# Weight sums for the seven products from GpSimd to VectorE, with a new issue order in all blocks of a fused attention and feed-forward kernel

## The chip, the cores and the metric

The kernel runs on one core of a Trainium2 chip. Time is device time of one execution in microseconds (us). The core has a matrix engine (TensorE, PE in the profile; its weight loads are listed apart as PEld), a vector engine (VectorE, DVE), a scalar engine (ScalarE, ACT), GpSimd (POOL) and a queue that issues transfers (SyncE, SP). Each engine works through its own instructions in order; an instruction that has to wait holds up what stands behind it on its engine.

## The reference

```python
for c in range(24):                    # chunks of 32 queries, each with a window of keys
    k_full = concat(mem_k, k[c*32-16 : c*32+40])      # 8 memory keys and up to 56 others
    v_full = concat(mem_v, v[c*32-16 : c*32+40])
    s = q[c*32 : c*32+32] @ k_full.T / sqrt(64)
    a = exp(s - max(s));  a = a / (sum(a) + 1e-9)
    out[c*32 : c*32+32] = a @ v_full
x = attention output as (4*768, 8*64) = (3072, 512)
h = x @ w_in                           # 512 x 2048
g = where(h >= 1, h, where(h <= -1, 0, (h + 1)**2 / 4))
result = g @ w_out                     # 2048 x 512
```

Everything is float32, with 4 batches, 8 heads, 768 positions and heads of 64.

## The kernel before

The 3072 rows are six blocks of 512 (`TB`). For a block, attention makes x, transposed; then for each of 16 slices `fc` of the hidden dimension one product gives h (in PSUM, from the pool `ps_h` with two buffers), ScalarE and VectorE make g of it, and a second product adds it into the block's four output banks (two pairs, tags `a0` and `a1`). To keep float32 accuracy, every operand of a product is split into a high part (a rounded copy, by ScalarE) and a low part (the remainder, a subtraction on VectorE), and three of the four products of parts are added.

Weights come as 64-bit words; `decode` (L184) makes float32 of a pair of slices and splits it: two instructions on ScalarE, four on VectorE, of 128x1024. There are 16 such decodes, `w0` to `w15`.

Attention of half a block (`attention`, L405; for block 0 `first_attention`, L248) is a chain: scores on TensorE into the PSUM pair with tag `s`, maximum and subtraction on VectorE, exp on ScalarE, normalisation and six transposes on VectorE, the product with the values on TensorE into the same pair `s`, then high and low part of x.

Blocks 0 and 1 use plain products: `half_step` (L438; 256 rows) and `step` (L479; 512 rows). A slice of `step` passes through: h on TensorE (12 matmuls of 512 columns), relus on ScalarE (three instructions), join on VectorE, high part on ScalarE, low part on VectorE, and two output halves of six matmuls each on TensorE.

Blocks 2 to 5 (`SECOND` is 2) form h with seven products of half-size operands in place of eight (Strassen's way), four slices at a time: `quad` (L765), with `product` (L665). For that, sums of the weights are needed, once for all blocks. `build(m)` (L563), for m from 0 to 7, makes them: two additions of 128x512 join the high and the low part again (`fef`), four subtractions of 128x256 give the sums (`tf`), ScalarE splits them (`st`, a high part of 128x1024), VectorE takes the low part, and a transfer stores `st` in device memory (`saved`), from where later transfers bring it into places of the weights that are no longer needed (`load_t`, L591). `fef` and `tf` use tag `f`, which has two buffers and serves `decode` and the output copies `ob` as well. The tile `st` has one buffer. In the kernel before, the six additions and subtractions of `build` run on GpSimd.

Nothing is ordered by a scheduler while it runs. The string `FIRST` (L27) is the order in which steps of all chains of blocks 0 to 1, of the decodes, the builds and the attention of blocks 0 to 2 are issued. Each token moves its chain by one step: `g0` to `g3` are the attention of block 0, `n0` and `n1` of block 1, `n2` and `n3` of block 2; `w` are decodes; `A` and `B` half steps of the halves of block 0, `E` its steps; `C`, `D` and `F` the same for block 1; `t` are builds; `+` issues the next load of the list `early`. `n1`, `E12` and so on in this text are such chains.

`QUADS` (L61) is the order within a quad of four slices, four quads to a block, the same for each of blocks 2 to 5. `p1` to `p7` are the products, 12 matmuls of 256 columns each into the PSUM bank X or Y; `c` copies X on ScalarE, `a` adds Y on VectorE, `r`, `m`, `h`, `l` are relus, join, high and low part for one of the four parts of g, `g` adds the part into the output (12 matmuls of 512 columns). A minus sign means the part of the quad before. `z0` and `z1` copy out the two output pairs of the block before (`store`, L519: one copy on VectorE, one on ScalarE, each with its transfer). `d` and `k` are sums and splits of x, `@S` starts the attention of half of the next block and `@V` issues its value product; `0` and `1` move these attention chains by one step. All instructions stay on their engine in the order of issue (`InOrder`, L81).

Of the kernel before, what the change touches and what calls it, by code (L numbers as in the profile page):

```python
# [25 lines left out]

FIRST = """  # L27
    + + g0 g0 g0 + g0 g1 g0 + g0 g0 g1 g1 g0 g1 + g1 g0 w0 g1 g1 + g1 g0 w0 g1 w0 + g0 g1 w0 w0 g2
    + g0 w0 g1 w1 g2 + g2 g1 g0 g3 g2 + g1 g2 A0 + g3 g2 g2 g3 g2 g3 A1 A0 + g2 g2 + g3 g3 w1 A1 w2
    g3 w1 w3 A0 g3 g2 w2 g3 + g3 w1 w2 g2 + g3 g3 g2 A0 g3 B0 w1 w2 w1 w4 A0 B0 w3 A1 B0 w2 + A2 B1  # L30
    A1 A2 B1 w2 A1 w3 A0 B1 B2 + w5 w3 B1 A2 B0 B0 B2 B1 w3 w4 A3 B2 + w3 A2 w7 A2 w4 B0 w5 A1 B2
    A2 w6 w4 w5 B3 A3 B2 w4 + B1 B2 w4 E4 + A3 B3 + w8 w6 + w9 A3 w5 w5 A3 w6 w10 B3 w11 w6 w5 w7
    B3 A3 + E4 + w6 B3 E5 E4 E5 E4 w13 w7 B3 w6 w7 E4 w8 w7 w12 + E6 E5 E4 E4 E7 E5 w8 w14 + E6 E5
    E5 E5 w7 w15 w8 w9 E6 w8 w9 E6 E6 E7 w9 E6 E7 w8 w9 E6 w9 E7 E7 E8 w10 E8 E9 w11 w10 w10 E8 w10
    E8 w11 E9 E7 E8 w11 w10 w11 E8 E9 E9 E8 w12 w12 w11 E9 E10 E10 E11 w12 E7 w13 E10 w12 E10 w13 +
    n0 E10 + E11 w12 E12 E10 E12 E10 n0 w14 w13 w13 n0 E11 n0 E9 w13 E9 E11 n0 E11 n0 E11 n0 n0 +
    n0 E13 n0 n0 n0 n0 E11 n0 w14 n0 E13 w15 E12 n0 w14 n0 w15 E12 n0 E14 E12 w14 E14 n1 w14 w15
    E12 w15 n1 E15 E13 n1 E14 E13 n1 E14 E13 n1 C0 E12 n1 w15 n1 E14 n1 C0 n1 n1 n1 E15 E13 n1 C1
    E15 E13 n1 E15 E14 C1 n1 E15 C1 C2 + C0 C2 C0 C2 C1 n1 C1 E14 n1 C0 n1 E15 n1 C2 E15 C0 E15 E15
    D0 E15 C1 D1 C3 E15 t0 D0 t0 t0 t0 D3 D0 D1 t0 C2 C3 D1 D0 D1 t0 t0 t1 D0 C3 D0 C3 t0 C3 t1 t1  # L40
    D2 F4 D1 t1 D3 D2 t1 t1 D3 t1 t2 C2 D1 D2 D2 C3 D3 F5 F4 t2 t2 t2 t1 t2 D2 D2 t2 D3 F6 F4 F4 t2
    t2 F5 F5 t3 t3 t3 F4 t3 t3 F5 D3 F6 F5 F6 F5 t3 t4 F6 t3 t3 t4 F5 t4 F7 t4 n2 t4 F4 t4 t5 t5 F7
    F4 t4 F7 n2 F6 t5 t5 t4 n2 F8 F7 t5 F7 F9 t5 F8 n2 F8 F6 t6 n2 t6 t6 t5 t6 F6 F9 F8 F7 t5 t6 F8
    F9 n2 t6 t7 F7 n2 + n2 n2 F11 n2 t6 t7 t6 t7 n2 t7 t7 n2 F10 n2 F11 F9 F9 n2 F10 t7 F10 F12 t7
    F8 n2 t7 + n2 F10 F8 F10 F11 F11 n3 F13 n3 F9 n2 n3 F12 F10 n3 F11 F12 + F10 n3 n3 F12 F9 n3 n2
    n3 n3 F11 F13 n3 n3 n3 F12 F11 F14 F13 F14 n3 F12 F12 F13 n3 n3 F15 n3 + F14 F13 n3 F15 F15 F15
    F13 F15 F14 F14 F13 n3
"""


# [28 lines left out]

# [887 lines left out]
```

## Time and profile before

| | us |
|---|---|
| median of three runs | 607.29 |
| lowest and highest | 606.29, 607.94 |
| the profiled execution | 606.56 |
| its span, first to last instruction | 604.8 |
| TensorE busy, of the span | 582.8 |
| VectorE busy | 388.5 |
| ScalarE busy | 332.4 |
| GpSimd busy | 55.0 |

The profile shows one execution. A busy engine need not be at its peak: matmuls overlap, so that TensorE counts as busy while the next matmul could already have started. What it loses is seen from the distance of the starts of neighbouring matmuls. The line of an instruction is nearly always L89, that of the helper that records it; the names of the tiles tell which step it is: `ps_h` is h, `ps_o` the output, `ps_s` scores, `ps_x` values, `gw`, `gt`, `gh`, `gl` the way from h to the parts of g, `fef`, `tf`, `st` the builds, `w`, `f`, `wr` the decodes, `pr`, `pt` the probabilities and their transposes.

### The profile page before, as it was taken

To read this page: it belongs to the slowest core of one execution; us is meant where nothing else is said; L and a number is where in the kernel's file an instruction comes from. 1 tells how busy PE (TensorE), PEld (TensorE's weight loads), DVE (VectorE), ACT (ScalarE), POOL (GpSimd) and SP (SyncE) were. 2 spreads that over 40 slices of the span, in tenths; PEclk is the share of its full clock that TensorE was granted. 3 is DMA by queue.
4 is the path that set the end of the run, shared out by engine and by line. 5 is a ranking of instruction groups with operands and counts; after the bars stand their busy time and mean duration, and the time that the engine had idled before them with its cause. 6 is when DMAs were issued, how large, how long until landed. Compare 5 with 4: busy or idle time off the path is not lost.

```text
span 604.8 us, 13956 instructions
## 1 busy us (share of the span) xinstructions
PE 582.8 (96%) x6072; PEld 503.7 (83%) x6072; DVE 388.5 (64%) x547; ACT 332.4 (55%) x587; POOL 55.0 (9%) x54
## 2 busy tenths in 40 slices
...
DVE  5789999995668777744657645557555557423332
...
GB/s 353 423 418 420 23 0 106 127 59 131 166 114 244 260 74 328 179 200 161 95 72 144 170 169 165 123 72 114 200 125 86 140 3 11 199 106 92 83 0 70
DMA packets 39437, 91.07 MB, mean 151 GB/s; under 512 B 2896, under 2 KB 29776, under 8 KB 33744
## 3 DMA queue, kind: packets, MB, share of 16 engines
...
q10 hardware_dynamic: 144, 0.13, 0.1%
q14 instruction: 14, 0.11, 0.1%
...
## 4 chain that ended last, share of the span: by engine, by line
PE 83%; DVE 9%; ACT 2%; DMA 2%; POOL 2%; issue 2%; ACTq 0%; DVEq 0%; POOLq 0%
PE ps_o L89 39%; PE ps_h L89 37%; PE ps_x L89 4%; PE ps_s L89 3%; DVE pt L89 1%; DMA saved<-st 1%; POOL tf L89 1%; DVE f L89 1%; DVE gl L89 1%; DVE pr L89 1%; ACT gw L89 1%; DVE st L89 1%; DVE gw L89 1%; DVE den L89 1%; DMA qk<-in_first_qk_dram 1%
## 5 line engine op out<-in xcount | busy, mean ns | idle before, releaser
L89 PE MATMUL ps_o<-wr,gh 128*128 128x512 f32 x768 | 242.2, 396 | 2.5 <-DVE ob L89 1.6
L89 PEld LDWEIGHTS ps_o<-wr,gh 128*128 128x128 f32 x768 | 139.1, 188 | 32.3 <-DVE ob L89 2.4
L89 PE MATMUL ps_o<-wr,gl 128*128 128x512 f32 x384 | 151.9, 396 | 1.2 <-DVE gl L89 1.2
L89 PE MATMUL ps_h<-s,wr 128*128 128x256 f32 x768 | 99.7, 282 | 0.0
L89 PEld LDWEIGHTS ps_h<-s,wr 128*128 128x128 f32 x768 | 96.4, 188 | 2.5 <-ACT u L89 0.2
L89 PE MATMUL ps_h<-xth,wr 128*128 128x512 f32 (+1 forms) x320 | 92.9, 365 | 0.7 <-ACT gt L89 0.7
L89 DVE SCALAR_TENSOR_TENSOR gw<-gw,gt 128x512 f32<-128x512 f32 (+1 forms) x88 | 61.3, 699 | 47.1 <-ACT gw L89 46.5
L89 PEld LDWEIGHTS ps_o<-wr,gl 128*128 128x128 f32 x384 | 72.2, 188 | 19.1 <-DVE gl L89 2.4
L89 DVE TENSOR_TENSOR gl<-gw,gh 128x512 fp32r<-128x512 f32 (+1 forms) x104 | 71.3, 694 | 24.4 <-ACT gh L89 24.1
L89 ACT CAST gh<-gw 128x512 fp32r<-128x512 f32 (+1 forms) x104 | 60.4, 586 | 33.6 <-DVE gw L89 33.6
L89 PEld LDWEIGHTS ps_h<-xth,wr 128*128 128x128 f32 x320 | 60.1, 201 | 10.5 <-ACT gt L89 1.1
L89 ACT ACTIVATE gw<-gw 128x512 f32<-128x512 f32 (+1 forms) x104 | 61.5, 591 | 0.0
L89 DVE TENSOR_TENSOR gt<-gt,ps_h 128x512 f32<-128x512 f32 x32 | 22.0, 688 | 58.8 <-ACT gt L89 35.9
L89 PE MATMUL ps_h<-xtl,wr 128*128 128x512 f32 (+1 forms) x160 | 56.8, 364 | 0.6 <-DVE xtl L89 0.6
L89 ACT ACTIVATE gw<-ps_h 128x512 f32<-128x512 f32 (+1 forms) x56 | 29.9, 535 | 48.7 <-PE ps_h L89 39.9
L89 ACT COPY gt<-ps_h 128x512 f32<-128x512 f32 x32 | 18.7, 585 | 65.7 <-PE ps_h L89 65.7
L89 PEld LDWEIGHTS ps_h<-sa,wr 128*128 128x128 f32 x384 | 48.4, 188 | 1.8
L89 PE MATMUL ps_h<-sa,wr 128*128 128x256 f32 x384 | 49.4, 282 | 0.0
L89 DVE STREAM_TRANSPOSE pt<-pr 32x512 f32<-32x512 f32 (+1 forms) x60 | 41.4, 700 | 1.3
L89 DVE SCALAR_TENSOR_TENSOR f<-w,f 128x1024 uint32<-128x1024 uint32 x32 | 38.9, 1220 | 0.2
L89 POOL TENSOR_TENSOR fef<-wr 128x512 f32<-128x512 f32 x16 | 25.0, 1582 | 140.2 <-DMA out_dram<-ob 139.6
L89 PEld LDWEIGHTS ps_h<-xtl,wr 128*128 128x128 f32 x160 | 32.6, 204 | 5.2 <-DVE xtl L89 0.8
...
## 6 DMA issues: line engine op xcount, KB each, us to landing
...
```

Of the source, the lines that this page charges most:

```text
L89: return self.tc.keep_in_program_order(getattr(self.engine, name)(*args, **kwargs))
```

## The change

The six additions and subtractions of `build` are issued on VectorE in place of GpSimd, in the same forms. `FIRST` holds the same tokens in another order, from its 41st token on; the builds' tokens, `t0` to `t7`, stand where their steps now run in VectorE's queue. `QUADS` holds the same tokens in another order in each of its four strings. Nothing else differs. The lines of `FIRST` are cut here; the part that is kept holds the attention of block 1 (`n0`, `n1`), the first builds and the place of `n2`.

```diff
 FIRST = """
...
-    E12 w15 n1 E15 E13 n1 E14 E13 n1 E14 E13 n1 C0 E12 n1 w15 n1 E14 n1 C0 n1 n1 n1 E15 E13 n1 C1
-    E15 E13 n1 E15 E14 C1 n1 E15 C1 C2 + C0 C2 C0 C2 C1 n1 C1 E14 n1 C0 n1 E15 n1 C2 E15 C0 E15 E15
-    D0 E15 C1 D1 C3 E15 t0 D0 t0 t0 t0 D3 D0 D1 t0 C2 C3 D1 D0 D1 t0 t0 t1 D0 C3 D0 C3 t0 C3 t1 t1
...
+    E10 w12 w13 n0 E10 w13 E11 + E12 E11 w13 n0 E9 w14 n0 E10 E11 w13 E12 n0 n0 E9 E10 E11 E11 E11
+    n0 n0 E12 n0 n0 n0 n0 + E13 n0 E12 n0 w14 E13 w15 E12 w14 n0 w15 n0 n0 E14 E12 n1 w14 n0 C0 w14
+    w15 n1 E13 E15 n1 E14 E12 w15 E13 E14 E13 n1 n1 n1 E14 w15 n1 C0 E15 E14 n1 + n1 E15 n1 E13 n1
+    n1 n1 C1 n1 C1 C0 E13 E15 C2 E14 E15 E14 C1 n1 E15 n1 C2 E15 C0 n1 n1 E15 E15 C0 D0 E15 C2 E15
+    C1 D1 C3 D0 C0 C1 t0 C2 D1 D3 t0 D0 C1 D0 t0 C3 t0 D2 t0 t0 t0 D0 F5 D1 C2 t0 t1 D3 t1 t1 C3 t1
...
+    t4 F5 t5 t5 t4 t5 t5 F7 t5 n2 t5 F7 F6 t6 t5 t6 t5 F8 F8 n2 n2 F8 n2 F7 t6 F9 t6 F9 n2 t6 t6 n2
+    t6 F8 t7 n2 F8 F10 F9 F9 F6 t6 t7 F11 n2 n2 n2 F7 t7 n2 n2 + F9 t7 n2 t7 F10 F8 F11 t7 F8 t7
...
 """
...
 QUADS = (
     """
-    @S0 p1 p2 -h12 -g22 c1 p6 a11 p5 0 dS4 r11 0 m11 -l12 0 -g12 c2 kS4 p7 -g21 c3 0 a22 r22 z0 h11
-    z1 0 0 m22 h22 l11 p4 p3 r21 0 a12 l22 r12 g11 m21 h21 l21 m12
+    @S0 -h12 p1 p2 -g22 0 -l12 c1 p6 a11 0 -g12 p5 r11 0 z0 dS4 c2 m11 p7 kS4 c3 h11 a22 0 -g21 r22
+    z1 m22 l11 h22 p4 r21 0 p3 a12 l22 0 0 r12 m21 h21 l21 g11 m12
     """,
     """
-    0 p2 -h12 0 p1 c1 a11 -g21 p6 -l12 r11 m11 0 0 c2 h11 -g22 p7 p5 0 0 c3 a22 @V0 r22 -g12 p4 p3
-    0 m22 h22 l22 l11 r21 a12 r12 @S1 g11 m21 h21 l21 m12
+    p1 -h12 p2 0 0 c1 a11 0 -g21 p6 c2 -l12 0 r11 m11 0 -g22 p7 p5 0 @V0 c3 -g12 a22 h11 r22 p4 p3
+    0 m22 h22 l11 a12 r12 g11 @S1 l22 r21 m21 h21 l21 m12
     """,
     """
-    1 1 p2 p1 -g22 c1 a11 r11 1 p6 m11 1 1 -h12 p5 -g21 c2 p7 -l12 c3 h11 -g12 a22 l11 r22 m22 1 1
-    h22 p4 l22 r21 p3 1 g11 m21 h21 1 a12 r12 m12 1 1 l21
+    1 p2 p1 c1 1 a11 -g22 r11 m11 1 1 1 p6 p5 -h12 c2 -g21 p7 -l12 -g12 c3 h11 a22 1 r22 l11 m22 1
+    h22 p4 l22 r21 p3 m21 h21 1 a12 r12 m12 1 g11 1 l21 1
     """,
     """
-    p1 1 -h12 -g22 c1 p2 p6 -g21 a11 c2 -l12 1 kA11 @V1 r11 p7 1 c3 m11 h11 kA12 p5 dS3 a22 -g12
-    dS1 r22 dS2 p4 p3 l11 m22 h22 l22 kA22 a12 r21 g11 m21 r12 kS2 kS1 h21 m12 l21 kS3
+    p1 p2 c1 1 p6 -g22 -g21 c2 a11 1 kA11 @V1 r11 kA12 1 -h12 p7 m11 -l12 h11 c3 p5 dS3 a22 p4 p3
+    dS1 r22 dS2 l11 m22 h22 -g12 g11 l22 a12 kA22 r21 m21 r12 m12 h21 kS3 kS2 l21 kS1
     """,
 )
...
         for j in range(2):
             hi, lo = (weights(0, 2 * m + j, part).bitcast(F32) for part in range(2))
-            pool.tensor_tensor(fef[:, j].rearrange("p a b -> p (a b)"), hi, lo, op=ALU.add)
+            dve.tensor_tensor(fef[:, j].rearrange("p a b -> p (a b)"), hi, lo, op=ALU.add)
             yield
...
-        pool.tensor_tensor(tf[:, 1], b12, b11, op=ALU.subtract)
+        dve.tensor_tensor(tf[:, 1], b12, b11, op=ALU.subtract)
         yield
-        pool.tensor_tensor(tf[:, 2], b22, b12, op=ALU.subtract)
+        dve.tensor_tensor(tf[:, 2], b22, b12, op=ALU.subtract)
         yield
-        pool.tensor_tensor(tf[:, 0], b22, tf[:, 1], op=ALU.subtract)
+        dve.tensor_tensor(tf[:, 0], b22, tf[:, 1], op=ALU.subtract)
         yield
-        pool.tensor_tensor(tf[:, 3], b21, tf[:, 0], op=ALU.subtract)
+        dve.tensor_tensor(tf[:, 3], b21, tf[:, 0], op=ALU.subtract)
         yield
```

More of the change, by code (lines that the diff above doesn't have):

```diff
@@ L28 @@
     + + g0 g0 g0 + g0 g1 g0 + g0 g0 g1 g1 g0 g1 + g1 g0 w0 g1 g1 + g1 g0 w0 g1 w0 + g0 g1 w0 w0 g2
[L29 to L37, printed above, removed]
-    E12 w15 n1 E15 E13 n1 E14 E13 n1 E14 E13 n1 C0 E12 n1 w15 n1 E14 n1 C0 n1 n1 n1 E15 E13 n1 C1
@@ L39 @@
-    E15 E13 n1 E15 E14 C1 n1 E15 C1 C2 + C0 C2 C0 C2 C1 n1 C1 E14 n1 C0 n1 E15 n1 C2 E15 C0 E15 E15
-    D0 E15 C1 D1 C3 E15 t0 D0 t0 t0 t0 D3 D0 D1 t0 C2 C3 D1 D0 D1 t0 t0 t1 D0 C3 D0 C3 t0 C3 t1 t1
-    D2 F4 D1 t1 D3 D2 t1 t1 D3 t1 t2 C2 D1 D2 D2 C3 D3 F5 F4 t2 t2 t2 t1 t2 D2 D2 t2 D3 F6 F4 F4 t2
-    t2 F5 F5 t3 t3 t3 F4 t3 t3 F5 D3 F6 F5 F6 F5 t3 t4 F6 t3 t3 t4 F5 t4 F7 t4 n2 t4 F4 t4 t5 t5 F7
-    F4 t4 F7 n2 F6 t5 t5 t4 n2 F8 F7 t5 F7 F9 t5 F8 n2 F8 F6 t6 n2 t6 t6 t5 t6 F6 F9 F8 F7 t5 t6 F8
@@ L44 @@
[L44 to L47, printed above, removed]
+    + g0 w0 g1 w1 g2 g1 g2 g3 + g0 g2 g1 A0 g2 g3 g2 g3 + g3 A1 A0 g2 + g2 + g3 g2 g3 + A1 w1 w2 g3
+    w1 g2 w3 A0 g3 + g3 w2 g3 w1 w2 g2 + g3 g2 g2 A0 g3 g3 A1 B0 + w2 w4 w1 w1 A0 B0 w3 + A2 B0 A1
@@ new lines @@
+    w2 B1 A1 A2 + w3 B0 w2 B1 B2 B1 w4 w3 B1 w5 A2 + B1 B0 w3 A0 A3 B0 w7 A2 A1 w4 w3 A2 B2 w5 B2
+    w6 w4 + B2 w5 B2 B3 B1 A3 E4 w4 A3 + w8 w4 + B3 w5 E5 B2 w9 + A3 + E4 w6 B3 w5 A2 w6 E4 w6 B3
+    A3 A3 w5 B3 w10 w6 w7 w11 E4 B3 w6 E5 w7 w8 + w7 E5 E7 w13 w7 E5 w12 E6 + w8 w14 E4 E6 w15 w7
+    E4 w8 w9 E6 E5 E8 E5 w9 w8 w9 E6 E7 E6 w9 E7 w9 E8 E5 w8 E6 E9 E7 E7 w10 w11 w10 E7 E8 E4 E9
+    w10 E8 w10 E6 E8 w11 w10 + w11 w12 w11 E9 E7 w12 E10 w11 E9 n0 E8 E9 E8 E10 w12 E10 E11 w13 w12
+    E10 w12 w13 n0 E10 w13 E11 + E12 E11 w13 n0 E9 w14 n0 E10 E11 w13 E12 n0 n0 E9 E10 E11 E11 E11
@@ new lines @@
+    n0 n0 E12 n0 n0 n0 n0 + E13 n0 E12 n0 w14 E13 w15 E12 w14 n0 w15 n0 n0 E14 E12 n1 w14 n0 C0 w14
+    w15 n1 E13 E15 n1 E14 E12 w15 E13 E14 E13 n1 n1 n1 E14 w15 n1 C0 E15 E14 n1 + n1 E15 n1 E13 n1
+    n1 n1 C1 n1 C1 C0 E13 E15 C2 E14 E15 E14 C1 n1 E15 n1 C2 E15 C0 n1 n1 E15 E15 C0 D0 E15 C2 E15
+    C1 D1 C3 D0 C0 C1 t0 C2 D1 D3 t0 D0 C1 D0 t0 C3 t0 D2 t0 t0 t0 D0 F5 D1 C2 t0 t1 D3 t1 t1 C3 t1
+    C3 t1 C3 D1 D0 t1 D2 F4 D3 D1 D2 D3 C3 D1 t1 t2 F6 t1 t2 C2 D3 t2 D3 t2 D2 D2 F4 F4 F5 t2 t2 t3
```

4 lines of the change are left out of this document (added).

## The prediction

> **What bounds the kernel now.** I read the page first, for which engine is full and where.
>
> ```profile
> span 604.8 us, 13956 instructions
> PE 582.8 (96%) x6072; PEld 503.7 (83%) x6072; DVE 388.5 (64%) x547; ACT 332.4 (55%) x587; POOL 55.0 (9%) x54
> DVE  5789999995668777744657645557555557423332
> ```
>
> TensorE (PE) is busy 96% of the span, so it can gain little and loses at once what is put in its way; VectorE (DVE) is full only up to the ninth slice (15.12 us each); GpSimd's (POOL's) 55 us are the sums that the change moves. Next, busy time by stretch.
>
> ```profile
> 45.00:94.00 49.00, 49.00 (x236) 39.56 (x243) 48.64 (x60) 39.03 (x62) 0.00 (x0) 1.00 0.34 140
> 94.00:137.00 43.00, 41.51 (x674) 34.70 (x670) 41.39 (x58) 21.16 (x41) 0.00 (x0) 1.00 0.32 110
> 137.00:210.00 73.00, 70.66 (x687) 56.84 (x686) 49.41 (x53) 36.40 (x69) 54.30 (x48) 1.00 0.45 176
> 210.00:300.00 90.00, 89.46 (x992) 78.43 (x992) 56.35 (x84) 48.24 (x85) 0.00 (x0) 1.00 0.56 181
> 300.00:590.00 290.00, 289.84 (x2852) 259.96 (x2851) 156.33 (x236) 161.84 (x288) 0.00 (x0) 1.00 0.35 108
> ```
>
> The columns are PE, weight loads, DVE, ACT (ScalarE), POOL, then clock and DMA. Three regimes: up to 137 us PE and DVE are both full (DVE 90.03 of 92 us); from 137 to 210 DVE has 23.6 us free while PE idles 2.34; behind 210 PE idles 0.54 in 90 and 0.16 in 290. So only what PE loses up to 210 can be won, and behind that the new `QUADS` can only lose. What PE loses stands in its timeline; a bracket is the idle time and what ended it.
>
> ```profile
> 113.72 1.10 PE L89 MATMUL ps_h<-xth,wr 128*128 128x512 f32 x4
> 115.86 1.47 PE L89 MATMUL ps_s<-qk 64*32 64x64 f32 x128 [1.04 <-issue]
> ...
> 131.54 0.48 PE L89 MATMUL ps_x<-pt,v 64*64 64x32 f32 x12
> 132.45 1.94 PE L89 MATMUL ps_x<-pt,v 64*64 64x32 f32 x116 [0.43 <-DVE pt L89]
> 134.32 0.50 PE L89 MATMUL ps_o<-wr,gh 128*128 128x512 f32 x1
> ...
> 138.37 0.40 PE L89 MATMUL ps_o<-wr,gl 128*128 128x512 f32 x1
> 138.77 0.73 PE L89 MATMUL ps_o<-wr,gh 128*128 128x512 f32 x2
> ...
> 147.47 0.72 PE L89 MATMUL ps_o<-wr,gh 128*128 128x512 f32 x2
> 148.52 0.50 PE L89 MATMUL ps_o<-wr,gl 128*128 128x512 f32 x1 [0.32 <-DVE gl L89]
> ...
> 166.17 0.40 PE L89 MATMUL ps_o<-wr,gl 128*128 128x512 f32 x1
> 166.99 0.73 PE L89 MATMUL ps_o<-wr,gh 128*128 128x512 f32 x2 [0.42 <-ACT gh L89]
> 168.62 0.50 PE L89 MATMUL ps_o<-wr,gl 128*128 128x512 f32 x1 [0.90 <-DVE gl L89]
> ...
> 194.08 1.10 PE L89 MATMUL ps_h<-xth,wr 128*128 128x512 f32 x4
> 195.87 0.50 PE L89 MATMUL ps_h<-xth,wr 128*128 128x512 f32 x1 [0.69 <-ACT gt L89]
> ```
>
> A matmul of 512 columns is followed by the next one after 0.23 us (x4 in 1.10, the last one's 0.40 included), so the loss is larger than the bracket: 113.72 + 4 x 0.23 = 114.65, and the next starts at 115.86, 1.21 us late. In the same way 148.52 is 0.48 late, 166.99 is 0.59, 168.62 is 1.06 and 195.87 is 0.86; the first matmul behind a wait takes 0.10 more than the pitch. The value product of 131.54 needs 2.78 us to the next work where its 128 small matmuls otherwise need 2.0 (1.94 for 116 of them), so 0.78. Sum: 4.98 us; with 138.77, which is 0.17 late without a bracket, and 0.10 for each of the five behind 137 us, 5.7. The last four, 3.4 us with their restarts, fall into the time of the sums.
>
> **The change part by part.** *The sums.* POOL loses 48 instructions, DVE gets them. First the prices while POOL works (window 141 to 201), POOL's own, and then the same forms without POOL (window 100 to 140).
>
> ```profile
> L89 DVE TENSOR_TENSOR st<-tf,st 128x1024 fp32r<-128x1024 f32 x7 | 10.4, 1492 | 8.0 <-ACT st L89 8.0
> L89 DVE SCALAR_TENSOR_TENSOR gw<-gw,gt 128x512 f32<-128x512 f32 x6 | 7.0, 1159 | 3.6 <-ACT gw L89 3.6
> L89 DVE TENSOR_TENSOR gl<-gw,gh 128x512 fp32r<-128x512 f32 x6 | 6.9, 1160 | 0.7 <-ACT gh L89 0.7
> L89 DVE SCALAR_TENSOR_TENSOR gw<-gw,gt 128x256 f32<-128x256 f32 x5 | 4.7, 955 | 4.5 <-ACT gw L89 4.5
> L89 DVE TENSOR_TENSOR gl<-gw,gh 128x256 fp32r<-128x256 f32 x6 | 4.5, 783 | 1.2 <-ACT gh L89 1.2
> L89 DVE TENSOR_REDUCE den<-pr 128x16 f32<-128x1024 f32 x1 | 1.2, 1207 | 0.0
> ...
> L89 POOL TENSOR_TENSOR fef<-wr 128x512 f32<-128x512 f32 x16 | 25.0, 1582 | 140.2 <-DMA out_dram<-ob 139.6
> L89 POOL TENSOR_TENSOR tf<-fef,tf 128x256 f32<-128x256 f32 x16 | 15.9, 995 | 0.6
> L89 POOL TENSOR_TENSOR tf<-fef 128x256 f32<-128x256 f32 x16 | 13.7, 879 | 4.4 <-DVE st L89 4.0
> ```
>
> ```profile
> L89 DVE TENSOR_TENSOR wr<-f,wr 128x1024 fp32r<-128x1024 f32 x3 | 3.7, 1220 | 0.0
> L89 DVE SCALAR_TENSOR_TENSOR gw<-gw,gt 128x512 f32<-128x512 f32 x5 | 3.4, 685 | 0.0
> L89 DVE TENSOR_TENSOR gl<-gw,gh 128x256 fp32r<-128x256 f32 x2 | 0.8, 422 | 0.2 <-ACT gh L89 0.2
> ```
>
> Added to DVE: 16 of 128x512 at 0.685 and 32 of 128x256 at 0.422, 11.0 + 13.5 = 24.5 us. Given back to DVE: with two operands from SBUF it takes 1.49 for 1.22, 1.16 for 0.685 and 0.96 or 0.78 for 0.42 while POOL works, a reduction with one operand takes its usual 1.21: 7 x 0.27 + 12 x 0.475 + 5 x 0.53 + 6 x 0.36 = 12.4 us. The stretch from 137 to 210 then holds 49.4 + 24.5 - 12.4 = 61.5 of 73 us on DVE, 84%. It fits, but in one queue: a sum now stands ahead of a `join` or `low`, and a sum that waits holds them up.
>
> [...]
>
> So three of the four late matmuls behind 137 (0.48, 0.59, 1.06, waits for `gl` and `gh` whose own rows were stretched) lose their cause, and the fourth (0.86: ACT's relus queued behind its `st` copy, which waited for POOL's `tf`) as well. What holds a `build` up then? Its `st` has one buffer, so the next ACT copy into it waits for the store to land.
>
> ```profile
> 335.22 0.59 ACT L89 COPY gt<-ps_h 128x512 f32<-128x512 f32 x1 [3.84 <-PE ps_h L89]
> ...
> L89 SPq DMA_DIRECT2D saved<-st x8: 319/320/327, 151.1 to 203.3; - x8
> DMA to landing us min/median/max: 3.8/4.3/4.9
> ```
>
> One round is 1.1 (an ACT copy of 128x1024, twice the first row's 0.59 or less) + 1.22 + 4.3 = 6.6 us, 8 rounds 53 us, inside the 60 us that POOL took; before, the stores ran 52.2 / 7 = 7.5 us apart. Then I add the rows up along both new queues. PE, behind `n1`'s values (they end near 134.4, below): up to `n2`'s values 20 output groups of six (1.40), 5 half and 9 whole `h` groups (1.43, 2.80), one set of scores (1.4) and some 0.3 of changes between shapes, 62 us: 196.4. DVE, behind `n1`'s last `lo` at 137.0: 52 us of rows up to `n2`'s last transpose and about 7.5 of waits (the first `fef` for the output store that frees tag `f`, as POOL's did, 1; `F4`'s relus 1.5; `st` copies that wait for a landing, 1 each): 196.5 to 196.9. The transposes are wanted 0.2 behind the first of those matmuls, so **0.5 us is lost** (bounds 0 and 2, one row of 1.22 and one of 0.685 more). Every `gl` on the way comes 1 to 10 us ahead of its `o` group.
>
> *The order up to 137 us.* DVE never idles, so moving an instruction ahead moves the rest by its row. `E12`'s join (0.61 back to back) now precedes `n0`'s transposes, so `n0.x` starts that much later: 0.6 lost. But `E12`'s first output half (6 x 0.23 = 1.4) precedes `n1`'s scores, which hides their 1.21, and `E14`'s second half (1.4) precedes `n1`'s values, which hides the 0.78. `n1`'s values so end near 134.4 where the trace has them and that half end at 134.32 + 1.5. In ACT and `ps_h` I find no wait over 0.5 us, and 0.6 would be absorbed at `n0.x`. First 36 us: only `g3`'s transposes and `g2`'s values change places, both behind the same ACT copies; 0, between -1 and +1.
>
> *QUADS.* One edit costs. In quad 0 `z0` moved from behind `r22` to ahead of `c2`: its ACT copy, ahead of `c2` in ACT's queue, waits for `-g12` and then for DVE's copy.
>
> ```profile
> ACT ob L89 <- DVE ob L89: 6.6, 3, 3.7
> ```
>
> From the start of `-g12`'s last matmul: 0.40 until it ends, DVE's copy 0.69, ACT's 0.59, `c2` 0.59: 2.3 us until `p7` may add to X; PE has 0.23 and `p5` (12 matmuls of 256 columns, half of 0.23 each: 1.4), so it stands 0.6, with restart 0.7. Three blocks (3, 4, 5; block 2 has no earlier one): **2.1 us lost**, 0 if the copies overlap, 3 at most. The other moves have 1 us or more of PE work between producer and user.
>
> Sum: 5.7 won (138.77, which waited for the output copies, too: `D` work now stands between), 0.6 + 0.5 + 2.1 lost: 2.5 us. The profiled execution took 606.56 (604.8 and 1.76 around it), 0.73 under the median of 607.29; 607.29 - 2.5 = **604.8**.
>
> **The rivals.**
> *Copies overlap, transposes in time:* the 0.5 and 2.1 are not lost: 607.29 - 5.1 = 602.2. Against it: ACT waited for DVE's `ob` three times.
> *The waits only move:* the 3.4 us of the sums' stretch come back at `n2`'s values, `n3`'s scores and the `ps_h` buffers, since ACT's relus stand behind `st` copies that wait 4.3 us for a store. Left is 2.5 - 3.4: 608.2, or 606.5 if half returns. For it: 84% in a queue in order; against: DVE worked at 98% from 45 to 137 with PE complete.
> *DVE becomes the bound (slower):* if its waits for ACT's `st` exceed the 11.5 us that are free (73 - 61.5), 1.4 us for each of 8 builds, PE follows DVE. Now DVE waits 8.0 us there (7 times). With 2 us each, 16 - 11.5 = 4.5 over: the 3.4 not won and 4.5 more, 607.29 - 2.5 + 3.4 + 4.5 = 612.7; with 1.6 us, 609.5. Against it: sums need nothing from ACT and fill such waits.
> *The clock:*
>
> ```profile
> 27.40:34.00 6.60, 4.25 (x144) 3.64 (x142) 4.80 (x6) 4.57 (x9) 0.00 (x0) 1.00 1.01 423
> 34.20:40.80 6.60, 6.01 (x28) 6.02 (x29) 6.33 (x10) 5.52 (x12) 0.00 (x0) 0.50 1.01 420
> ```
>
> After 6.6 us with PE busy 4.25 the granted clock was 0.50 for the next 6.6. The reordered transposes lie in that first window. If a second one were halved, 3.3 us: 608.1; if the first were not, DVE still bounds until 137, 0. [...]
>
> **How the numbers follow.** Forecast (603 to 606) 0.55, overlap 0.12, waits move 0.20, DVE bound 0.09, clock 0.04. A measurement here can tell 0.3%, 1.8 us, from no change. Faster (under 605.5): 0.48 of the first and the 0.12, 0.60. Slower (over 609.1): 0.09 and a little of the clock, 0.11. Within: 0.29. The range takes in overlap and half-returned waits, and the ends of the unknown costs: 601.5 to 607.6; outside it are DVE's bound, the clock and the worst of the moved waits.
>
> **What would show it.** After: POOL empty from 141 to 201; `gl` and `gw` of 128x512 at 0.69 throughout; DVE 60 to 63 of the 73 us; no PE wait for `gl` there; `n1`'s scores and values without a bracket; a wait of about 0.6 at `p7` once in each of blocks 3 to 5, ended by ACT; 0.6 more at `n0.x`. Wrong if PE waits for `gt` or `pt` by more than 1.5 us between 137 and 225, or if DVE idles over 11.5 us there on `st`.

## The result and the profile after

The kernel after takes 599.5 us (median of 4 runs, 599.33 to 600.18) against 606.79 for before beside it (605.89 to 607.94): ratio 0.988, interval 0.986 to 0.990. The gain is 7.3 us; forecast were 2.5, and the time lies below the range that was given. The profiled execution took 599.33 us, its span is 597.6.

The page of after, the busy time of the engines, and below it its windows (columns as in the prediction):

```profile
span 597.6 us, 13941 instructions
PE 579.3 (97%) x6072; PEld 501.4 (84%) x6072; DVE 395.5 (66%) x595; ACT 333.0 (56%) x587; POOL 0.7 (0%) x6
DVE  5899999988889776735765735765735564523332
```

```profile
45.00:94.00 49.00, 48.97 (x338) 39.48 (x337) 48.82 (x60) 37.39 (x61) 0.00 (x0) 1.00 0.43 172
94.00:137.00 43.00, 42.93 (x570) 36.02 (x569) 39.81 (x57) 22.25 (x43) 0.00 (x0) 1.00 0.26 94
137.00:210.00 73.00, 73.00 (x697) 59.83 (x696) 62.96 (x110) 39.08 (x74) 0.00 (x0) 1.00 0.48 184
210.00:300.00 90.00, 90.00 (x1118) 79.67 (x1118) 55.13 (x82) 48.83 (x86) 0.00 (x0) 1.00 0.52 165
300.00:590.00 290.00, 287.85 (x2730) 256.76 (x2723) 153.31 (x231) 159.56 (x283) 0.00 (x0) 1.00 0.36 109
```

TensorE now works 73.00 of 73 us while the sums are made, and VectorE's load there is 62.96 us. Of the stretches shown, only the last has lost more than 0.1 us of TensorE, 2.15 of 290. The groups of instructions of VectorE in 141 to 201 us (count, busy time and mean of one, idle time before them) give the prices:

```profile
L89 DVE TENSOR_TENSOR st<-tf,st 128x1024 fp32r<-128x1024 f32 x8 | 9.8, 1222 | 1.3 <-ACT st L89 1.2
L89 DVE TENSOR_TENSOR fef<-wr 128x512 f32<-128x512 f32 x14 | 9.2, 682 | 0.1
L89 DVE TENSOR_TENSOR tf<-fef,tf 128x256 f32<-128x256 f32 x16 | 6.7, 420 | 0.2
L89 DVE TENSOR_TENSOR gl<-gw,gh 128x512 fp32r<-128x512 f32 x7 | 4.8, 687 | 0.5 <-ACT gh L89 0.4
```

A sum costs VectorE 0.68 and 0.42 us, `gl` is back at 0.69 from 1.16, and VectorE waits for ACT's `st` 1.3 us in all where it waited 8.0.

To see where the 7.2 us of span come from, one number per place is enough: TensorE's **lag**, the time at which a piece of its work starts less the sum of what the pieces ahead of it in its own list take unhindered (1.43 us for a half `h` group, 2.80 for a whole one, 1.40 for an output group, and so on, as in the prediction). It grows by every wait and by every half-clock spell. It is worked out in the same way for each profiled run (us). A row is one execution; that of before_start_after (608.28) lies 2.9 above the median of its kernel, that of after_pool (607.56) 1.0.

| run | `E8.h` | `n1.x` | `F4.h` | `n2.x` | last half of `F13` | span |
|---|---|---|---|---|---|---|
| before | 23.48 | 24.57 | 26.19 | 28.93 | 28.60 | 604.8 |
| after | 21.61 | 21.53 | 21.32 | 21.22 | 20.65 | 597.6 |
| after_pool | 22.21 | 22.15 | 25.47 | 26.28 | 28.38 | 605.5 |
| before_dve | 23.72 | 24.80 | 25.83 | 26.59 | 26.65 | 602.8 |
| before_start_after | 21.67 | 23.12 | 24.54 | 28.95 | 28.37 | 606.1 |
| after_start_before | 23.20 | 23.12 | 22.91 | 22.81 | 22.42 | 599.2 |
| before_pt_late | 21.80 | 23.26 | 24.86 | 27.54 | 26.94 | 603.3 |
| before_warm | 21.48 | 22.91 | 24.51 | 28.37 | 27.94 | 603.4 |
| after_z0 | 21.27 | 21.19 | 20.98 | 20.88 | 20.36 | 594.9 |

Between the first two rows: 1.87 us come before `E8` (68 to 77 us), 1.17 between `E8` and `n1`'s values, 4.67 from there to `n2`'s values, 0.24 up to `F13`, 7.95 in all, and 0.75 are given back behind it. The prediction had 0 for the first and 2.1 lost for the last.

The medians of all runs (us, median of 4 to 12 runs of each; before beside them had medians of 606.0 to 606.7):

| run | time | ratio to before, interval |
|---|---|---|
| after_pool | 606.53 | 0.9988, 0.9964 to 1.0011 |
| before_dve | 605.11 | 0.9966, 0.9943 to 0.9990 |
| after_start_before | 601.28 | 0.9914, 0.9880 to 0.9949 |
| before_start_after | 605.38 | 0.9987, 0.9959 to 1.0014 |
| before_pt_late | 604.90 | 0.9966, 0.9947 to 0.9985 |
| before_warm | 605.49 | 0.9984, 0.9964 to 1.0004 |
| after_warm | 600.52 | 0.9901, 0.9877 to 0.9926 |
| after_again | 599.65 | 0.9886, 0.9864 to 0.9908 |
| after_z0 | 597.64 | 0.9864, 0.9837 to 0.9891 |
| after_quads_before | 599.53 | 0.9898, 0.9870 to 0.9925 |
| before_shift | 610.47 | 1.0064, 1.0045 to 1.0084 |
| after_z0_shift | 612.45 | 1.0081, 1.0056 to 1.0107 |
| before_shift13 | 607.85 | 1.0007, 0.9989 to 1.0025 |
| after_z0_shift13 | 598.99 | 0.9872, 0.9854 to 0.9890 |

### The profile page after: what moved, and what is told of

Same layout as the page of the kernel before. It is cut to its first block, busy times and chain, and to the rows that moved or that the text cites. A ratio compares the mean times of both kernels' runs of the same rounds, so it can differ in the third digit from the quotient of the medians.

```text
span 597.6 us, 13941 instructions
## 1 busy us (share of the span) xinstructions
PE 579.3 (97%) x6072; PEld 501.4 (84%) x6072; DVE 395.5 (66%) x595; ACT 333.0 (56%) x587; POOL 0.7 (0%) x6
## 4 chain that ended last, share of the span: by engine, by line
PE 83%; DVE 11%; ACT 3%; issue 2%; DMA 1%; DVEq 0%
PE ps_o L89 40%; PE ps_h L89 36%; DVE f L89 4%; PE ps_x L89 4%; PE ps_s L89 3%; DVE wr L89 2%; DVE gw L89 1%; DVE gl L89 1%; ACT w L89 1%; DVE pr L89 1%; DMA qk<-in_first_qk_dram 1%; DVE pt L89 1%; DVE ob L89 1%; DVE den L89 1%; ACT gw L89 0%
## 5 line engine op out<-in xcount | busy, mean ns | idle before, releaser
L89 DVE SCALAR_TENSOR_TENSOR gw<-gw,gt 128x512 f32<-128x512 f32 (+1 forms) x88 | 56.0, 638 | 56.1 <-ACT gw L89 55.7
L89 PE MATMUL ps_h<-xth,wr 128*128 128x512 f32 (+1 forms) x320 | 91.4, 360 | 0.0
L89 DVE TENSOR_TENSOR gl<-gw,gh 128x512 fp32r<-128x512 f32 (+1 forms) x104 | 66.8, 643 | 23.4 <-ACT gh L89 23.1
L89 ACT CAST gh<-gw 128x512 fp32r<-128x512 f32 (+1 forms) x104 | 60.7, 589 | 35.1 <-DVE gw L89 34.9
L89 PEld LDWEIGHTS ps_h<-xth,wr 128*128 128x128 f32 x320 | 58.7, 197 | 9.8 <-ACT gt L89 0.5
L89 ACT ACTIVATE gw<-gt 128x512 f32<-128x512 f32 x32 | 20.2, 633 | 28.9 <-DVE gt L89 28.9
```

Source lines behind the costliest of these rows:

```text
L89: return self.tc.keep_in_program_order(getattr(self.engine, name)(*args, **kwargs))
```

## The experiments

### Which engine, which order

**after_pool** is after with the sums back on GpSimd:

```diff
-            dve.tensor_tensor(fef[:, j].rearrange("p a b -> p (a b)"), hi, lo, op=ALU.add)
+            pool.tensor_tensor(fef[:, j].rearrange("p a b -> p (a b)"), hi, lo, op=ALU.add)
...
-        dve.tensor_tensor(tf[:, 3], b21, tf[:, 0], op=ALU.subtract)
+        pool.tensor_tensor(tf[:, 3], b21, tf[:, 0], op=ALU.subtract)
```

> The kernel after with the sums put back on GpSimd and its new orders kept. Theory E (the lock between GpSimd and VectorE made the late gl and gh of 137 to 210 us): the two-operand rows of VectorE are stretched again (gw of 128x512 near 1.1 us instead of 0.69) while GpSimd works its 55 us, TensorE waits for gl and gh again, 3 to 4 us are given back: 602.5 to 604. Theory O (the new order alone removes these waits): 599.5, within 1 us.

Measured: 606.53, so 7.0 us are given back, all that the change had won. TensorE's timeline from 140 to 225 us holds three long waits:

```profile
147.21 0.53 PE L89 MATMUL ps_h<-xth,wr 128*128 128x512 f32 x1 [1.73 <-ACT gt L89]
184.83 0.50 PE L89 MATMUL ps_h<-xth,wr 128*128 128x512 f32 x1 [0.66 <-ACT gt L89]
200.29 1.94 PE L89 MATMUL ps_x<-pt,v 64*64 64x32 f32 x116 [0.86 <-DVE pt L89]
```

Two of them name ACT's `gt` and one VectorE's `pt`; none names `gl`. ACT's and VectorE's groups in 141 to 201 us of the same run say why:

```profile
L89 ACT CAST st<-tf 128x1024 fp32r<-128x1024 f32 x7 | 7.4, 1050 | 18.4 <-POOL tf L89 17.2 <-DMA saved<-st 1.2
```

```profile
L89 DVE TENSOR_TENSOR gl<-gw,gh 128x512 fp32r<-128x512 f32 x6 | 6.3, 1070 | 0.9 <-ACT gh L89 0.9
L89 DVE TENSOR_REDUCE den<-pr 128x16 f32<-128x1024 f32 x1 | 1.2, 1221 | 0.5 <-ACT pr L89 0.5
```

ACT stands 17.2 us ahead of its `st` copies for GpSimd's sums, and the relus that TensorE needs stand behind it. VectorE's rows are stretched as theory E said (1.07 for 0.69), but the waits come through ACT. The waits have a second price, in the clock; the windows around the first one:

```profile
144.00:147.50 3.50, 1.77 (x14) 1.57 (x13) 0.87 (x1) 1.91 (x4) 3.34 (x5) 1.00 0.00 0
147.60:150.90 3.30, 3.30 (x9) 2.59 (x8) 2.83 (x4) 1.50 (x5) 3.22 (x4) 0.50 0.68 278
```

Right behind the wait the granted clock is 0.50 for 3.4 us, 1.7 us of work lost with TensorE complete at 3.30 of 3.30. A second such spell begins at 202.2. So theory E holds in its result (the engine matters) and misses in the path and in the size: 7.0 instead of 3 to 4. Theory O falls. The lag says where: at `n1.x` this run is still 2.4 us ahead of before (22.15 against 24.57), and by `F13` the builds have taken that away (28.38 against 28.60).

**before_dve** is the other half, before's order with the sums on VectorE:

```diff
-            pool.tensor_tensor(fef[:, j].rearrange("p a b -> p (a b)"), hi, lo, op=ALU.add)
+            dve.tensor_tensor(fef[:, j].rearrange("p a b -> p (a b)"), hi, lo, op=ALU.add)
...
-    D3 D2 t1 t1 D3 t1 t2 C2 D1 D2 D2 C3 D3 F5 F4 t2 t2 t2 t1 t2 D2
+    D3 D2 t1 t1 D3 t1 t2 C2 D1 D2 D2 C3 D3 F5 F4 t2 t1 t2 t2 t2 D2
```

and likewise at `t4`/`t5` and `t5`/`t6`: before's order as it stands cannot run with the sums on VectorE, for the reason given below.

> The kernel before with the sums on VectorE and its own orders kept, but for three builds (1, 4 and 5) whose low part is issued ahead of the third sum of the next one, because that sum takes the buffer that the low part reads. Theory E: the waits of 148 to 196 us go, the start and the order up to 137 us stay as they were: 3 to 4 us less than before, 603 to 604, VectorE 61 to 63 us busy in 137 to 210. Theory O or moved waits: sums ahead of joins and low parts hold up TensorE elsewhere in that stretch, 606 to 608.

Measured: 605.11, 1.3 less than before (0.6 to 3.5 by the interval). In the profiled run the lag from `n1.x` to `n2.x` grows by 1.79 where before's grew by 4.36, so 2.6 us of the stretch's waits are gone, and two stay:

```profile
167.28 0.50 PE L89 MATMUL ps_o<-wr,gl 128*128 128x512 f32 x1 [0.71 <-DVE gl L89]
198.69 1.94 PE L89 MATMUL ps_x<-pt,v 64*64 64x32 f32 x116 [0.35 <-DVE pt L89]
```

Theory E's direction is right, its 3 to 4 us are too many: in before's order VectorE's queue now holds up `gl` and `pt`. Together: the new order alone is worth 0, the new engine alone 1.3, both 7. Neither part has a share of its own: the new order spaces the steps by VectorE's 0.68 and 0.42 us a sum, and GpSimd needs 1.58 and 0.88 to 1.0 for them in before. That this spacing is what makes the two belong together fits ACT's 17.2 us, but no run tests it alone.

### The first 43 us

Both orders have issued the same steps after 87 tokens, so the two beginnings can be exchanged. **after_start_before** takes them from before, **before_start_after** the other way round:

```diff
-    + g0 w0 g1 w1 g2 g1 g2 g3 + g0 g2 g1 A0 g2 g3 g2 g3 + g3 A1 A0 g2 + g2 + g3 g2 g3 + A1 w1 w2 g3
-    w1 g2 w3 A0 g3 + g3 w2 g3 w1 w2 g2 + g3 g2 g2 A0 g3 g3
+    + g0 w0 g1 w1 g2 + g2 g1 g0 g3 g2 + g1 g2 A0 + g3 g2 g2 g3 g2 g3 A1 A0 + g2 g2 + g3 g3 w1 A1 w2
+    g3 w1 w3 A0 g3 g2 w2 g3 + g3 w1 w2 g2 + g3 g3 g2 A0 g3
```

> The kernel after with the first 87 steps in the order of before (both orders have issued the same steps by then; only what lies near 24 to 36 us differs). Theory S (the first 42 us hold 2.1 us of the gain, and it is kept to the end): 601.6, a spell of 6.8 us of half clock near 34 us again, TensorE's first output group of block 0 near 41.8 us instead of 41.1. Theory D (VectorE bounds up to 137 us, as the prediction had it): 599.5, within 0.5.

> The kernel before with the first 87 steps in the order of after. Theory S: 2.1 us less than before, 604.7, with a half-clock spell of 3.4 us instead of 6.8 near 34 us. Theory D: 606.8, within 0.5, the 2 us lost again before 137 us.

Measured: 601.28, 1.8 us more than after's 599.5, as theory S said (the clock spell was 3.4 us, not 6.8); the intervals of the two ratios overlap (0.9880 to 0.9949, 0.9861 to 0.9901), so that the lag is the firmer evidence. The lag of this run is 1.6 above after's at `E8` and 1.8 above it at `F13`: what the start loses is kept to the end. The mirror gives 605.38, 1.05 less than before with an interval that holds 0; its lag is 1.8 us under before's at `E8` and 1.65 at `F4`, and then lost in the builds, where in the profiled execution, one of the slowest, a wait and a half-clock spell at 168 us follow. In time it is inconclusive; in the trace up to 150 us it is theory S. Theory D, that VectorE bounds this stretch and the gain is lost by 137 us, falls twice: in before_start_after VectorE's instructions between 50 and 137 us, in the order of before, all start 1.45 us earlier than there.

What in the start? **before_pt_late** moves two tokens of before, `g2`'s ACT copy behind `w2`'s scaling and `g2`'s values behind `g3`'s copy:

```diff
-    ... A1 A0 + g2 g2 + g3 g3 w1 A1 w2    g3 w1 w3 A0 g3 g2 w2 g3 + g3    w1 w2 g2
+    ... A1 A0 + g2    + g3 g3 w1 A1 w2 g2 g3 w1 w3 A0 g3    w2 g3 + g3 g2 w1 w2 g2
```

> The kernel before with two tokens moved: the ACT copy of group 2's transposes stands behind the scaling of w2 (so behind A1's relus too) instead of ahead of them, and group 2's values stand behind the copy of group 3's transposes. Theory A (in before ACT waits 1.4 us for the transposes of group 2, and w2's scaling, which VectorE waits for 1.79 us, stands behind it): A3's first product starts 19 us behind A0's instead of 21.3, as with the whole new order of the first 87 steps; 1.5 to 2 us less than before in time. Rival K (the length of the half-clock spell alone made the difference): 20.5 to 21.3 us, and it goes with the spell.

**before_warm** keeps before's order and fills TensorE's idle time; **after_warm** does the same in after, with 3, 2 and 1:

```diff
+    def fill(n):
+        for _ in range(n):
+            pe.matmul(both["x3"][:, 0], warm[:, 0:P], warm, start=True, stop=True)
...
             pe.transpose(ps[:, n * P : (n + 1) * P], pr[:, 2 * n : 2 * n + 2, :], ident)
+        if g == 2:
+            both["x3"] = two_banks("s", "ps_x")
+        if g > 1:
+            fill({2: 2, 3: 6}[g])
         yield
...
-        ps = two_banks(PLACES[g][1], "ps_x")[:, :, 0:HT]
+        ps = (both.pop("x3") if g == 3 else two_banks(PLACES[g][1], "ps_x"))[:, :, 0:HT]
```

> The kernel before with eight matmuls of 512 columns more on the tile of zeros, two behind the transposes of group 2 and six behind those of group 3, in idle time of TensorE up to 32.7 us; the orders stay. Theory K (the half clock costs TensorE's own time): no spell at 34 us, A3's first product 1.5 us or more earlier, 19.8 us behind A0's or less. Rival A (ACT's order holds the start up, the clock runs beside it): 20.3 to 21.3 us.

> The kernel after with six matmuls of 512 columns more, on the tile of zeros and into banks that the next value product overwrites: three behind the transposes of group 2, two behind those of group 3, one behind the values of group 2, into idle time of TensorE between 28.6 and 32.2 us. Theory C (the half clock behind that gap costs TensorE's own time): no half-clock spell behind 27 us, two products of 12 matmuls at 1.44 us instead of 2.5 and 1.8, 1.5 to 1.7 us less than after, 597.9. Theory D (VectorE bounds up to 137 us): within 0.5 of after.

One number tells these apart: the time from the start of `A0`'s first product to that of `A3`'s, with the same work between them in all runs. The window from the one to the other, of before, of before_pt_late and of before_warm (length, busy times, granted clock):

```profile
23.32:44.60 21.28, 18.29 (x216) 17.28 (x215) 18.14 (x29) 14.78 (x30) 0.00 (x0) 0.84 1.01 422
```

```profile
23.98:42.73 18.75, 16.26 (x216) 14.80 (x215) 17.21 (x28) 13.77 (x28) 0.00 (x0) 0.89 1.01 421
```

```profile
23.46:42.35 18.89, 17.40 (x223) 15.11 (x223) 17.11 (x28) 13.78 (x28) 0.00 (x0) 0.91 1.01 421
```

The granted clock of these three rows can't be compared: the profile of before has no record of the clock ahead of 27.29 us, and 1.00 stands there. TensorE's own matmuls tell the clock; three groups of five equal ones from before's timeline:

```profile
25.19 1.27 PE L89 MATMUL ps_h<-xth,wr 128*128 128x256 f32 x5
...
36.45 1.27 PE L89 MATMUL ps_h<-xth,wr 128*128 128x256 f32 x5
...
44.12 0.76 PE L89 MATMUL ps_h<-xth,wr 128*128 128x256 f32 x5
```

The second lies in the half-clock spell and the third behind it, so the first, as slow as the second, ran at half the clock too. In the runs of the table below TensorE is at half the clock when `A0` begins (its matmuls of 256 columns start 0.21 us apart, and 0.12 behind that), up to a time between 26 and 29 us that differs from run to run (26.4 in after_warm, 27.0 in after, 28.1 in before_pt_late) and moves `A0` to `A3` by some tenths. The last column therefore counts from `B0`'s product on, which starts behind the values of `g3`.

| run | order of the start | half-clock spell behind 28 us | `A0` to `A3` | `B0` to `A3` |
|---|---|---|---|---|
| before, before_dve | before | 6.8 | 21.28, 21.31 | 10.84, 10.83 |
| after_start_before | before | 3.4 | 20.55 | 9.60 |
| before_warm | before, gap filled | none | 18.89 | 8.73 |
| before_pt_late | two tokens moved | none | 18.75 | 8.62 |
| before_start_after, after_again | after | none | 18.88, 19.08 | 8.60, 8.93 |
| after, after_z0 | after | 3.4 | 19.03, 18.85 | 9.20, 9.14 |
| after_warm | after, gaps filled | none | 18.49 | 8.95 |

In before_warm ACT's and VectorE's order is that of before, `w2` is as late as there, and yet the 2.4 us are won as soon as the spell is gone, 2.1 of them from `B0` on: theory K. TensorE's timeline shows what was filled, before above, before_warm below:

```profile
32.69 1.14 PE L89 MATMUL ps_x<-pt,v 64*64 64x32 f32 x64 [1.67 <-ACT pt L89]
34.78 0.58 PE L89 MATMUL ps_h<-xtl,wr 128*128 128x256 f32 x1 [0.64 <-DVE xtl L89]
```

```profile
32.56 1.13 PE L89 MATMUL ps_x<-pt,v 64*64 64x32 f32 x64 [0.40 <-ACT pt L89]
34.64 0.38 PE L89 MATMUL ps_h<-xtl,wr 128*128 128x256 f32 x1 [0.63 <-DVE xtl L89]
```

The value product starts 0.13 earlier (0.27 counted from `A0`), no more; the clock makes the rest. Moving two tokens does as much, for with `g3`'s transposes ahead of `g2`'s values the one gap of 1.67 falls apart into smaller ones. So the order is the cause and the clock the means: before's order leaves the gap and had a spell in each of the five profiles with that gap; after's order has smaller gaps, and in eight profiles with it or with the two tokens moved the spell was absent (five) or 3.4 us long (after_z0_shift aside, below: it waits 3.06 and 2.63 us at 18 and 25 us, and its matmuls are still 0.21 us apart at 32). In after nothing more is won by filling (8.95 from `B0` on, as in after_again without a spell; the time, 600.5, is not less than after_again's): there the spell of 3.4 us costs only some 0.25 (9.20 against 8.93), because without it the products of that stretch wait for VectorE (0.34 us for `xtl` at 34.9 in after_warm). Behind before's start the same 3.4 us cost 0.9 (9.60 against 8.73). Theory A is thus right in naming the tokens and wrong in why; theory C falls for after. In time, before_pt_late won 1.3 us of the 1.5 to 2, and before_warm 0.7 with an interval that holds 0, because more was lost in the builds (its lag grows by 5.46 from `n1.x` to `n2.x`).

### The quads

**after_again** is after itself. **after_z0** moves one token, **after_quads_before** puts before's four quads into after:

```diff
-    @S0 -h12 p1 p2 -g22 0 -l12 c1 p6 a11 0 -g12 p5 r11 0 z0 dS4 c2 m11 p7 kS4 c3 h11 a22 0 -g21 r22
+    @S0 -h12 p1 p2 -g22 0 -l12 c1 p6 a11 0 -g12 p5 r11 0 dS4 c2 z0 m11 p7 kS4 c3 h11 a22 0 -g21 r22
```

> The kernel after itself, on the chip of the next three, to stand them against: 599.5, within 1 us.

> The kernel after with one token of quad 0 moved: z0 (copy and store of the last block's first half) stands behind c2 instead of ahead of dS4 and c2. Theory Z (c2 behind z0's ACT copy is what p7 waits for): the three waits of 0.61 at p7 with 0.1 of restart each are gone, 2.1 us less than after, 597.4. Rival (the wait moves to c3, or to z1 and the output product that needs its banks): within 0.6 of after.

> The kernel after with the four quads of before. Theory Z: the three waits at p7 go (2.16 us), the waits of before near 240, 273 and 365 us (0.18, 0.78, 0.37) come back: 0.8 less than after, 598.7. Rival (the new quads as a whole save more than the p7 waits cost): 600 or more.

After's timelines of TensorE, ACT and VectorE, at `p7` in block 3:

```profile
323.13 1.60 PE L89 MATMUL ps_h<-s,wr 128*128 128x256 f32 x12
325.18 1.68 PE L89 MATMUL ps_h<-s,wr 128*128 128x256 f32 x12 [0.45 <-ACT u L89]
```

```profile
324.06 0.59 ACT L89 COPY ob<-ps_o 128x512 f32<-128x512 f32 x1 [3.90 <-DVE ob L89]
324.54 0.59 ACT L89 COPY u<-ps_h 128x512 f32<-128x512 f32 x1
```

```profile
323.33 0.69 DVE L89 COPY ob<-ps_o 128x512 f32<-128x512 f32 x1 [4.83 <-PE ps_o L89]
```

This is the chain of the prediction, link by link: VectorE's copy of the output, ACT's copy, `c2` (the copy into `u`), `p7`. `p5` runs on from 323.13, its successor would follow at 324.57 and comes at 325.18, 0.61 late; the same stands at 418.23 and 509.69. In after_z0 `c2` is at 320.26 and `p5` and `p7` are one run:

```profile
322.84 3.04 PE L89 MATMUL ps_h<-s,wr 128*128 128x256 f32 x24
```

It takes 597.64, 2.0 less than after_again (599.65), with intervals of the ratios that overlap; the span less the lag at `F13` is 2.4 us shorter in its profile (574.5 against 576.9). Theory Z holds, and this is the fastest of the kernels run. after_quads_before does without them too: 574.7 in the same measure, theory Z's chain again; its time, 599.53, does not show it, as its profiled start is 0.7 later and it has one run at 602.8. What failed of its expectation is instructive: the waits of before near 240, 273 and 365 us did **not** come back with before's quads.

### The waits named "issue"

Before stands still at these two places without any named releaser; TensorE's timeline of before:

```profile
272.52 0.50 PE L89 MATMUL ps_o<-wr,gh 128*128 128x512 f32 x1
273.53 0.51 PE L89 MATMUL ps_o<-wr,gh 128*128 128x512 f32 x1 [0.52 <-issue]
...
364.14 1.28 PE L89 MATMUL ps_s<-qk 64*32 64x64 f32 x105
365.58 0.42 PE L89 MATMUL ps_s<-qk 64*32 64x64 f32 x23 [0.16 <-issue]
```

The second one is inside a run of 128 score matmuls that have all their data. Among the DMA queues is one named instruction. Its row for the whole span of before (packets, MB, share of 16 engines), and below it the row for the window 271.2 to 271.5 us; from 266.9 to 271.2 the queue has none:

```profile
q8 instruction: 47, 0.77, 0.5%
```

```profile
q8 instruction: 1, 0.02, 19.7%
```

0.77 MB in 47 transfers are 16 KB each; 6072 matmuls and as many weight loads over 47 are 258 instructions each, which points to TensorE's own instructions, in blocks of about 256 by this estimate (matmuls 349 and 3025, where before stands still, are 21 blocks of 127.4 matmuls and as many weight loads apart); 128 score matmuls with their weight loads would use up such a block in the 1.4 us that they take. The transfer begins at 271.3, and TensorE goes on at 273.5, 2.2 us later. **before_shift** tests this with 76 small matmuls in idle time at 8 us; **after_z0_shift** does the same on after_z0:

```diff
         ps = ps_h.tile([P, 512], F32, name="ps_h")
+        for n in range(76 if g == 0 else 0):
+            pe.matmul(ps[0:32, 0:64], warm[0:64, 0:32], warm[0:64, 0:64], start=True, stop=True)
         for n in range(NG // 2):
```

> The kernel before with 76 small matmuls on the tile of zeros ahead of group 0's transposes, in 4 us in which TensorE waits; nothing else. Every later instruction of TensorE stands 152 places further in its list. Theory I (the waits named issue at matmuls 349, 3025 and 4041, behind or in runs of 64 to 128 small score matmuls, are waits for TensorE's own instructions, whose transfers of the queue named instruction start 2.2 to 2.4 us before such a wait ends): the two waits near 272 and 365 us (0.8 to 1.4 and 0.4 to 1.6) go or move to another matmul, and so does the one in group 3's scores; the wait of 1.21 ahead of n1's scores, which VectorE ends, stays. Rival (they wait for data): all stay at the same work.

> The kernel with z0 behind c2, with the same 76 small matmuls. Theory I: the wait of 1.4 us within group 3's scores goes, and the start is up to 1 us shorter: 596.6 to 597.6, if no new wait of this kind arises. Rival: the start waits for other work, 597.6, within 0.5.

The waits at that work are gone in before_shift, as theory I said:

```profile
275.42 1.48 PE L89 MATMUL ps_s<-qk 64*32 64x64 f32 x128
276.83 0.72 PE L89 MATMUL ps_o<-wr,gh 128*128 128x512 f32 x2
```

But others come, behind matmuls 477, 1369 and 2263 of the list (349 plus 128 times 1, 8 and 15, less a few), and the kernels are 4 and 15 us slower. The longest is in after_z0_shift, behind a run of 128 scores:

```profile
210.48 0.39 PE L89 MATMUL ps_h<-xth,wr 128*128 128x512 f32 x1
214.83 0.80 PE L89 MATMUL ps_h<-xtl,wr 128*128 128x512 f32 x1 [3.96 <-issue]
```

The transfer for it lies at 212.6, again 2.2 us before TensorE goes on, and behind it matmuls of 512 columns start 0.43 us apart where 0.23 is usual, as at the granted clock of 0.50 in after_pool. Theory I holds in that the waits moved when the list was shifted; the hope of a shorter start fell (at 477, in `A0`'s first product, TensorE stands idle for 2.63 us). A small shift, **before_shift13** and **after_z0_shift13**, has `13` for `76` in the same lines:

> The kernel before with 13 small matmuls on the tile of zeros ahead of group 0's transposes, instead of 76: every later instruction of TensorE stands 26 places further. Theory I (a wait arises where the next 256 instructions begin right behind a run of small matmuls, less than the 2.2 to 2.4 us after the last such place that their transfer needs): the place moves from matmul 3025 back to 3012 of the old count, the stretch between two places then holds some 13 products of 0.12 us more, 1.5 us, and the waits near 272 and 365 us (0.8 to 1.6, 0.4 to 1.6) are gone or under 0.3. The place of matmul 349 falls on 336, where TensorE waits 1.2 us for VectorE anyway, so A0's first product starts up to 1 us earlier than 23.3. In time 1 to 2 us less than before. Rival (the place of the pages has no part): both waits stay, 606.

> The kernel with z0 behind c2, with the same 13 small matmuls. Theory I: the waits of 1.2 and 1.4 us ahead of and within group 3's scores fall together, up to 1 us less, 596.6 to 597.6, if no page falls badly elsewhere. Rival: 597.6, within 0.5; a new wait named issue would make it more.

```profile
272.61 1.38 PE L89 MATMUL ps_s<-qk 64*32 64x64 f32 x116
274.42 0.33 PE L89 MATMUL ps_s<-qk 64*32 64x64 f32 x12 [0.43 <-issue]
```

This is TensorE's timeline of before_shift13. In before the wait came 129 matmuls behind the start of the scores, now it comes 116 behind it, 13 earlier, and 13 were added: in both, 3025 matmuls of TensorE's list are done when it stands still. It falls on a place in the list, not on the work. But it is still 0.63 us long, not under 0.3; the one at 365 is gone.

Between before and after_quads_before the wait goes with how far ahead the transfer begins. In the latter the same scores have the same place in the list as in before, matmuls 2897 to 3024, and nothing waits:

```profile
264.16 1.48 PE L89 MATMUL ps_s<-qk 64*32 64x64 f32 x128
265.57 0.72 PE L89 MATMUL ps_o<-wr,gh 128*128 128x512 f32 x2
```

There the transfer begins at 263.1, 2.8 us before the second of these output matmuls; in before it began at 271.3, and the same matmul was due 1.5 us later. Why it begins earlier is not shown. In time before_shift13 wins nothing (607.85), and after_z0_shift13 is not better than after_z0 (598.99 against 597.64): it starts 0.4 us earlier and gets new waits of 0.6 and 0.7 at 143 and 145 us, which name ACT's `gt`.

## Why the prediction was wrong

**The sums: right.** GpSimd empty, sums at 0.68 and 0.42 for 0.685 and 0.422, VectorE 62.96 us of 73 for 61.5, `gl` at 0.687, all four late matmuls of the stretch gone. `gl` took 1.16 in before and 1.07 in after_pool while GpSimd worked and 0.687 in after without it, with the one-operand reduction at 1.21 to 1.22 in all three. That a lock between the two engines is behind this, as theory E has it, is the author's reading; no run shows more than these rows. What the prediction did not see is that the other path, ACT behind GpSimd's `tf`, costs more once the order is the new one: 17.2 us of ACT's time in after_pool.

**`n1`'s scores and values: right.** Both brackets are gone from TensorE's timeline of after, for the reason given, and `n0`'s values start without the 0.6 that was feared:

```profile
107.47 2.43 PE L89 MATMUL ps_x<-pt,v 64*64 64x32 f32 x128
114.22 1.48 PE L89 MATMUL ps_s<-qk 64*32 64x64 f32 x128
129.89 2.07 PE L89 MATMUL ps_x<-pt,v 64*64 64x32 f32 x128
```

**`n0.x` (0.6) and `n2.x` (0.5): two terms too many.** The lag does not grow at either (21.61 at `E8`, 21.53 at `n1.x`, 21.22 at `n2.x`), nor in after_start_before with its later start (23.20, 23.12, 22.81). The first took VectorE's row of 0.61 in front of the transposes for a delay of TensorE; the second came from adding up two queues over 60 us with an error of the size of the result. From `E8` to the end of `F13` the prediction's terms make 4.6 won; 6.1 were measured.

**The start: the step that failed.** "First 36 us: only `g3`'s transposes and `g2`'s values change places, both behind the same ACT copies; 0, between -1 and +1", and of the clock, "if the first were not, DVE still bounds until 137, 0". Measured: 1.9 us won, of which after_start_before, given before's start, loses 1.8 at the end. The swap broke up the gap of 1.67 us behind which the clock was halved, and VectorE did not hold the rest in place: in before_start_after its rows up to 137 us moved forward with TensorE, by 1.45. That VectorE was busy 90.03 of 92 us was read as a bound that an earlier start could not shift; it was a full queue that starts as soon as its work does. before_warm shows the clock's part with the order unchanged: 18.89 for 21.28 us.

**The quads: right in the term, wrong in the sum.** 2.1 us were foretold at `p7`, ended by ACT, in blocks 3 to 5; 3 x (0.61 + 0.11) = 2.2 stand there. But "behind that the new `QUADS` can only lose" was wrong: before's 0.78 at 273 and 0.37 at 365 us went too. They were not waits of the quads: after_quads_before has before's quads and neither wait. They go with the place in TensorE's list (3025 in before and in before_shift13) and with how early the transfer of instructions begins (2.2 us ahead of the matmul in before, 2.8 in after_quads_before), and neither stands in the prediction's terms, so this gain was unforeseen. Net 0.75 lost instead of 2.1.

So of the 4.7 us between the terms and the two spans, 1.9 are the start, 1.5 the two feared waits and small ones on that way, 1.35 the part behind `F13`, 1.15 of it the two instruction waits. Of the rivals, "waits only move" and "DVE becomes the bound" did not come about. Of "copies overlap, transposes in time" the second half did, and the copies did not overlap. The clock, priced at 3.3 us lost or nothing won, is what the start was won by.

Open: when a wait halves the clock (below), and how much of before's spread from run to run (604.7 to 611.4 us in one set) is half-clock spells behind waits.
